# Attention and a two-layer MLP in one kernel: the first batch's up units spread over its bursts, left output halves first, stores by halves, and v ahead of half a weight

## The chip, the cores and the metric

The kernel runs on one core of a Trainium2 chip. A core has a matrix engine (PE, TensorE; PEld is its weight load), a vector engine (DVE), a scalar engine (ACT), a general engine (POOL, GpSimd) and a queue engine (SP, SyncE). Each works through its own list of instructions in order; semaphores hold one engine back for another. DMA transfers are issued from SP, ACT or POOL and run on 16 DMA engines that all queues share. The metric is the device time of one execution in microseconds (us), as the median of several runs.

## What is computed

There are 8 batches, 12 heads, 448 tokens and a head width of 64; q, k and v come as float32 and the output is float32.

```python
q_n, k_n = rmsnorm(q, g_q), rmsnorm(k, g_k)      # over the head width
scores = matmul(q_n, k_n.T) / sqrt(64)
attn = exp(scores - max); attn = attn / (sum(attn) + 1e-9)
x = matmul(attn, v)                              # -> (8*448, 12*64) = (3584, 768)
h = x @ w_in                                     # w_in (768, 2048)
g = maximum(h, 0) + alpha * minimum(h, 0)        # alpha per column of h
out = g @ w_out                                  # w_out (2048, 768)
```

## The kernel before, in words

The twelve heads of a batch are split in two halves g of six, which lie on the lower and the upper 64 partitions. A pair y is two heads (`par`) of each half, four heads in all: y = 0 to 23, three pairs to a batch (G = 3). The 448 tokens are 7 blocks of 64 keys (J = 7). A tile (y, j) is one block of keys of one pair against all queries.

*Preparing a pair.* `load_qk(y)` (L95) loads q and k of a pair on the SP queue into `nat` (six buffers, so three pairs). `square` (L139; ACT for the first two pairs, then POOL), `reduce` (L149, DVE) and `root` (L157, ACT) give the inverse root mean square, `scale` (L166; POOL, some on DVE) multiplies and casts to fp16. Then the block is transposed: for pairs 0 to 5 by PE into PSUM and copied by DVE (`turn`, L186), from pair 6 on by a DMA transpose on SP (`turn_dma`, L176), after which `turn` only multiplies k by the gain on DVE (L190).

*Attention.* `score(y, j)` (L223) makes eight matmuls of 64 rows by 32 columns on parts of the array, into one of two `sc` buffers in PSUM. `soft` (L240, ACT) takes the exponential with a constant bias, no maximum. `den` (L265) sums the exponentials over keys with a matrix of ones, and `attv` (L281) multiplies them with v; both run through `over_keys` (L248) for a couple of pairs (y, y+1) or for the third pair alone, 56 matmuls of 64x32 each; for two pairs, `attv` runs twice. `log` and `invert` (ACT) make the reciprocal of the sum, and DVE multiplies (L306, L308) into `xT`.

*MLP.* `up(b, ft)` (L340) is one of 16 column blocks of the first layer for a batch: six matmuls 128x128x448, an ACT scaling by alpha (L350), a DVE maximum (L351) into `gT`. For batch 0 the first four units are begun early by `begin` (L331). `down(b0, t, oh)` (L355) is one half (oh = 0 left, 1 right) of the 768 output columns for 128 tokens: 16 matmuls 128x128x384, then a DVE copy into `osb` (L371). The output of a token tile is stored after its second half, by two DMAs on SP (L377).

*Banks.* PSUM gives two `sc` tiles (two banks each), one tile `acc` of two banks (den, attv, PE transposes of pairs 3 to 5, and up or down units marked `spare`), and two single banks `mm`.

*Order.* The program is written out in bursts, numbered n, by a planner that runs when the kernel is built. It cuts the 168 tiles into bursts of two, or three in bursts marked `late` (L416), and decides which burst holds a `den` (`den_at`) or `attv` (`av_at`). The lists `prep` and `post` (`at`, `after`, L433, L436) place loads, squares and reduces before or after a burst. From the costs UP = 1.13, DOWN = 2.6 and `cost(n)` (L488) it then deals out up and down units into the `gaps` of the bursts (L499 to L530): a unit is added to a burst until the clock of the costs passes the burst's even share. For batch 0 only the up units count toward that share (`mlp`, L507), and units shorter than UP are never cut short (L528). Of the six down units of batch 0 (three token tiles), four follow in its own period, left half and right half of a tile in turn.

The main loop (L587) then emits, per burst: `prep`; the scores and exponentials; `den` or `attv`; the third tile; roots, scales and DMA transposes; `log` and `invert`; the units of the gap, some of them in the spare bank (L640); `post`. In a burst with plain tiles the second exponential is emitted only after the first up unit (`wait`, L603). Burst 10 is `lead`: there `den` and `attv` of pair 2 come first, then the tiles of pair 3, with the begun up units of batch 0 between.

Weights come over POOL's queue: four parts of `w_in` after bursts 0, 5, 7, 8; the left half of `w_out` (two DMAs of 768 KB) after burst 10 and the right half after burst 11 (L583); v of batch 1 is asked for in burst 12 (L471). POOL issues them in order with its squares and scales.

Of the kernel before, what the change touches and what calls it, by code (L numbers as in the profile page):

```python
# [9 lines left out]
FP32 = mybir.dt.float32  # L10
FP16 = mybir.dt.float16
# [10 lines left out]
def kernel(  # L22
# [12 lines left out]
    nc = tc.nc  # L35
# [35 lines left out]
    nc.vector.memset(expb, EXP_BIAS)  # L71
    epsb = cst.tile([128, 1], FP32, name="epsb", tag="epsb")
    nc.vector.memset(epsb, RMS_EPS)
    ones = cst.tile([128, 32], FP16, name="ones", tag="ones")
    nc.vector.memset(ones, 1.0)
    ident = cst.tile([128, 128], FP16, name="ident", tag="ident")
    make_identity(nc, ident)
# [145 lines left out]
    def score(y, j):  # L223
        qT, kT = qkT[y, "q"], qkT[y, "k"]
        sc = pss.tile([128, 2, 512], FP32, name="sc", tag="sc")
        for c in range(2):
            for par in range(2):
                for g in range(2):
                    nc.tensor.matmul(  # L229
                        out=sc[ds(64 * g + 32 * c, 32), par, :S].rearrange(  # L230
                            "p (j c) -> p j c", j=J
                        ),
                        lhsT=kT[ds(64 * par, 64), j, g, ts(c, 32)],
                        rhs=qT[ds(64 * par, 64), :, g, :],
                        start=True,
                        stop=True,
                    )
        scs[y, j] = sc
# [8 lines left out]

    def over_keys(accs, ys, weights):  # L248

        if len(ys) == 2:  # L250
            heads = [(y, par, 0) for y in ys for par in range(2)]
        else:
            heads = [(ys[0], par, c) for par in range(2) for c in range(2)]
        for j in range(J):
            for h, (y, par, c) in enumerate(heads):
                for g in range(2):
                    nc.tensor.matmul(  # L257
                        out=accs[g][ds(32 * h, 32), :S],
                        lhsT=weights(g, y, par, c, j),
                        rhs=expT[y][ds(64 * g, 64), j, par, :],  # L260
                        start=(j == 0),
                        stop=(j == J - 1),
                    )

    def den(ys):  # L265
        dn = psa.tile([128, 2, 512], FP32, name="dn", tag="acc")
        over_keys(
            (dn[:, 0], dn[:, 1]), ys, lambda g, y, par, c, j: ones[ds(64 * g, 64), :]
        )
        rden[ys] = dn  # L270

# [9 lines left out]
    def attv(ys, half, spare=False, jobs=()):  # L281

        b, i = divmod(ys[0], G)
        v2 = vt[b].rearrange("p h j (d e) -> p h j d e", e=2)

        def weights(g, y, par, c, j):
            h = 2 * (y - G * b) + par
            if len(ys) == 1:
                return vt[b][ds(64 * g, 64), h, j, ts(c, 32)]
            return v2[ds(64 * g, 64), h, j, :, half]  # L290

        if half:
            av, accs = None, [psf.tile([128, 512], FP32, name="avb", tag="mm") for _ in range(2)]
        else:
            pool, tag = (pss, "sc") if spare else (psa, "acc")
            av = pool.tile([128, 2, 512], FP32, name="av", tag=tag)
            accs = (av[:, 0], av[:, 1])
        over_keys(accs, ys, weights)
        for f in jobs:
            f(ys)  # L300
        if b not in xT:
            xT[b] = att.tile([128, 2, G, S], FP16, name="xT", tag="xT")
        x, r = xT[b][:, :, i + half, :], rden[ys]
        if half:
            for g in range(2):
                nc.vector.tensor_mul(out=x[:, g], in0=accs[g][:, :S], in1=r[:, g])  # L306
        else:
            nc.vector.tensor_mul(out=x, in0=av[:, :, :S], in1=r)  # L308
# [41 lines left out]
        nc.scalar.activation(out=ah, in_=hT[:, :S], func=AF.Copy, scale=alpha_sb[:, ft : ft + 1])  # L350
        nc.vector.tensor_max(out=gT[:, ft, ds((b & 1) * S, S)], in0=hT[:, :S], in1=ah)  # L351

    osb = {}

    def down(b0, t, oh, jobs=(), spare=False):  # L355

        op = bank("op", spare)
        for ft in range(NF):
            nc.tensor.matmul(  # L359
                out=op[:, :OH],  # L360
                lhsT=gT[:, ft, ts(t, 128)],
                rhs=w_out_sb[:, ft, ds(oh * OH, OH)],
                start=(ft == 0),
                stop=(ft == NF - 1),
            )
        for f, a in jobs:
            f(*a)
        if oh == 0:
            osb[b0, t] = ffn.tile([128, DM], FP32, name="osb", tag="osb", bufs=2)
        o = osb[b0, t]  # L370
        nc.vector.tensor_copy(out=o[:, ds(oh * OH, OH)], in_=op[:, :OH])  # L371
        last = (b0, t) == (B - 2, J - 1)
        if oh == 1 or last:
            cols_out = ds(oh * OH, OH) if last else slice(None)
            for half in range(2):
                bb, j = divmod(2 * t + half, J)
                (nc.scalar if last and half else nc.sync).dma_start(  # L377
                    out=out4[b0 + bb, j, :, cols_out], in_=o[ds(64 * half, 64), cols_out]
                )

    def spin(count):

# [17 lines left out]
    while m < NG * J or steps:  # L400
        n = len(bursts)
        while steps:
            ys, values = steps[0]
            if values:

                if n in dens and ys != (G - 1,):
                    break
                avs[n] = ys
                av_at.update((y, n) for y in ys)
            else:  # L410
                if n in avs or any(last_in.get(y, n) >= n for y in ys):
                    break
                dens[n] = ys
                den_at.update((y, n) for y in ys)
            steps.pop(0)
        late = len(avs.get(n, ())) == 2 or any(y >= G for y in dens.get(n, avs.get(n, ())))  # L416
        bursts.append([])
        while len(bursts[n]) < (3 if late else 2) and m < NG * J:
            y, j = divmod(m, J)
            if j == 0 and y >= EB and av_at.get(y - EB, n) == n:  # L420

                if y - EB not in av_at:
                    break
                split[n] = min(len(bursts[n]), 2)
            bursts[n].append((y, j))
            first_in.setdefault(y, n)
            if j == J - 1:
                last_in[y] = n
            m += 1
# [17 lines left out]
    for y in range(G, NG):  # L447

        early = y < G + 2
        if early:  # L450
            n = turn_at[y - 1] + (y == G)
        elif y == G + 2:
            n = den_at[G - 1]
        elif y == 2 * G:
            n = turn_at[y] - 4
        elif y == 2 * G + 1:
            n = den_at[G] - 1
        elif y % G:
            n = den_at[y - 3 if y % G == 1 else y - G]
        else:  # L460
            n = av_at[y - 4]
        at(n - (6 if early else 5), load_qk, y)
        for nm in "qk":
            (after if early else at)(n - 2, square, y, nm)
            if early:
                after(n, reduce, y, nm)
            else:
                jobs.setdefault(n, []).append((reduce, (y, nm)))
        roots[n + 1] = y
# [7 lines left out]
    for b in range(B):  # L477
        ups = [(UP / 3 if b == 0 and ft < 4 else UP, up, (b, ft)) for ft in range(NF)]
        odd = b % 2
        new = [  # L480
            (DOWN, down, (b - odd, t, oh))
            for t in (range(3, J) if odd else range(3)) for oh in range(2)
        ]
        tail = len(new) if b == B - 1 else 4 if b == 0 else 2 if odd else 1
        periods.append((ups, carry, new[:tail]))
        carry = new[tail:]
# [12 lines left out]
    for b in range(B - 1):  # L499
# [4 lines left out]
        if b == 0:  # L504

            stop -= len(new)
            mlp = sum(u[0] for u in ups)  # L507
        per = (mlp + sum(cost(n) for n in range(lo, stop))) / (stop - lo)
        clock = 0.0
        for n in range(lo, hi):  # L510
            clock += cost(n)
            free = True
            while ups or old or new:
# [11 lines left out]
                ahead = 0.5 * (UP if ups else DOWN)  # L525
                if not (ups or old) and n + len(new) < hi:
                    break
                short = n in turns and len(gaps[n]) < 2 or u[0] < UP  # L528
                if n < stop - 1 and not short and clock + ahead > per * (n - lo + 1):
                    break  # L530
    ups, old, new = periods[B - 1]
    rest = []
# [47 lines left out]
    after(7, load_w_in, 2)  # L580
    after(8, load_w_in, 3)
    for c in range(4):
        after(first + c // 2, load_w_out, c)  # L583
    roots[3] = 2

    since = 2
    for n in range(NB):  # L587
# [2 lines left out]
        tiles = bursts[n]  # L590

        lead = n == den_at[G - 1]
        if lead:
            den(dens[n])
            attv(avs[n], 0, True, (log, invert))
        first_tiles = tiles[: split.get(n, 2)]
        for t in first_tiles:
            score(*t)
            if lead and t == tiles[0]:
                begin(1)  # L600
                begin(2)
        plain = lead or n not in dens and n not in avs
        wait = plain and not lead and gaps[n] and gaps[n][0][0] is up  # L603
        if lead:
            begin(3)
        for t in tiles[:1] if wait else first_tiles:
            soft(*t)
        if n in dens and not lead:
            den(dens[n])
# [23 lines left out]
        done = 0  # L633

        spare_at, clock = [], 0.0
        taken = n + 1 in dens or n + 1 in avs
        for k, (f, a) in enumerate(gaps[n]):
            free = 2.3 if n in dens else (0.1, 1.2, 0.0)[len(avs.get(n, ()))]
            since += 1
# [73 lines left out]
```

## Time and profile before

| | |
|---|---|
| median of 7 runs | 443.62 us (439.07 to 445.33) |
| the profiled execution | 441.08 us |
| its span, first to last instruction | 439.3 us, mean granted clock of PE 0.996 |
| PE busy | 416.2 us, 5381 matmuls and as many weight loads |
| ACT, DVE, POOL busy | 277.7, 211.9, 176.0 us |
| DMA | 53.89 MB, mean 123 GB/s |
| exponential of one tile (L243) | 1.005 us, 168 of them |
| up unit, down unit on PE (chain of work) | 1.13 us, 2.60 us |

Times in a profile count from the span's first instruction. A row of a timeline gives the start, the length, the engine (PEq, SPq and so on for an engine's queue), the line, the operation, the tile written and the tiles read, and in square brackets the idle time before it and what ended it; "issue" stands for a wait that the profile puts down to nothing else. A busy PE is not a PE at its peak. In part 2 of the page each digit is the busy share of one fortieth of the span in tenths.

### The profile page before, as it was taken

How to read it: one execution, taken by the hardware profiler on the slowest of the kernel's cores; microseconds unless marked ns; L12 is line 12 of the kernel's file. 1: busy time of each engine (PE TensorE's matmuls, PEld its weight loads, DVE VectorE, ACT ScalarE, POOL GpSimd, SP SyncE). 2: the span in 40 equal slices, each digit the busy share in tenths (PEclk: the TensorE clock that was granted, in tenths of full speed). 3: DMA queues.
4: the chain of work that ended last, by engine and by line, in shares of the span. 5: the costliest groups of instructions: out<-in, count | busy, mean ns of one | idle time of the engine just before them, and what ended most of it. 6: DMA issues, size and time to landing. Idle time of an engine off the chain costs nothing.

```text
span 439.3 us, 12178 instructions
## 1 busy us (share of the span) xinstructions
PE 416.2 (95%) x5381; PEld 215.1 (49%) x5381; DVE 211.9 (48%) x303; ACT 277.7 (63%) x385; POOL 176.0 (40%) x133
## 2 busy tenths in 40 slices
PE   7877888999997999999999999999999999999996
PEld 3334334454454545554554545554555545555563
DVE  3655655365664356445545356445544253333421
ACT  4895788578875687767746587767747586222300
POOL 5799793847273631556153632556043000000000
PEclk9899999999999999999999999999999999999999
DMA  8999999988327961678119751775118201111122
GB/s 210 231 207 221 161 248 196 175 170 204 85 60 118 214 161 39 122 183 210 36 28 221 153 154 39 126 181 126 36 27 167 67 2 37 39 36 37 36 73 72
DMA packets 65909, 53.89 MB, mean 123 GB/s; under 512 B 36528, under 2 KB 62400, under 8 KB 65856
## 3 DMA queue, kind: packets, MB, share of 16 engines
q1 hardware_dynamic: 51136, 40.19, 38.3%
q0 software_dynamic: 13984, 11.81, 18.4%
q10 hardware_dynamic: 736, 1.11, 1.0%
q8 instruction: 42, 0.69, 0.7%
q14 instruction: 11, 0.09, 0.1%
HBM read 45.62 MB, written 11.01 MB: 129 GB/s over the span
## 4 chain that ended last, share of the span: by engine, by line
PE 75%; DMA 9%; issue 5%; ACT 4%; DVE 3%; POOL 2%; SPq 2%; POOLq 0%; DVEq 0%; ACTq 0%
PE op L359 25%; PE hT L323 17%; PE hTa L323 9%; PE sc L229 7%; PE opa L359 5%; DMA vt<-in_v_dram 4%; PE dn L257 4%; PE av L257 4%; ACT expT L243 3%; DMA nat<-in_q_dram 2%; PE avb L257 2%; DMA kT<-qs 2%; DMA nat<-in_k_dram 1%; POOL qs L169 1%; SPq L103 1%
## 5 line engine op out<-in xcount | busy, mean ns | idle before, releaser
L243 ACT ACTIVATE expT<-sc,expb 128x896 f16<-128x896 f32 x168 | 160.8, 1005 | 35.8 <-PE sc L229 34.6
L359 PE MATMUL op<-w_out_sb,gT 128*128 128x384 f16 x736 | 127.1, 326 | 0.8 <-issue 0.8
L169 POOL TENSOR_TENSOR qs<-nat,rr 128x896 f16<-128x896 f32 x44 | 76.9, 1766 | 126.3 <-ACT rr L164 96.2
L359 PEld LDWEIGHTS <-gT 128*128 128x128 f16 x896 | 84.6, 98 | 67.6 <-issue 14.0
L323 PEld LDWEIGHTS <-w_in_sb 128*128 128x128 f16 x768 | 73.0, 98 | 75.5 <-issue 11.8
L323 PE MATMUL hT<-xT,w_in_sb 128*128 128x448 f16 x516 | 108.8, 353 | 0.4 <-DVE gT L351 0.4
L350 ACT ACTIVATE ah<-hT,cols 128x448 f16<-128x448 f32 x86 | 54.4, 634 | 55.5 <-PE hT L323 55.5
L146 POOL TENSOR_TENSOR sq<-nat 128x896 f32<-128x896 f32 x44 | 73.5, 1687 | 37.4 <-DMA nat<-in_q_dram 18.5
L351 DVE TENSOR_TENSOR gT<-hT,ah 128x448 f16<-128x448 f32 x86 | 53.6, 624 | 63.3 <-ACT ah L350 63.1
L229 PE MATMUL sc<-qT,kT 64*32 64x448 f16 x1344 | 54.1, 356 | 8.4 <-ACT expT L243 5.6
L371 DVE COPY osb<-op 128x384 f32<-128x384 f32 x46 | 25.6, 556 | 71.2 <-PE op L359 71.2
L323 PE MATMUL hTa<-xT,w_in_sb 128*128 128x448 f16 x240 | 51.9, 352 | 2.5 <-DVE xT L308 2.5
L152 DVE TENSOR_REDUCE ss<-sq 128x14 f32<-128x896 f32 x48 | 50.0, 1076 | 7.0 <-ACT sq L144 6.1
L350 ACT ACTIVATE ah<-hTa,cols 128x448 f16<-128x448 f32 x40 | 25.4, 635 | 30.9 <-PE hTa L323 30.9
L351 DVE TENSOR_TENSOR gT<-hTa,ah 128x448 f16<-128x448 f32 x40 | 25.0, 624 | 25.5 <-ACT ah L350 25.5
L229 PEld LDWEIGHTS <-kT 64*32 64x32 f16 x1344 | 15.7, 89 | 39.1 <-issue 34.1
L359 PE MATMUL opa<-w_out_sb,gT 128*128 128x384 f16 x160 | 27.7, 326 | 0.0
L257 PEld LDWEIGHTS <-vt 64*32 64x32 f16 x1344 | 19.7, 93 | 14.6 <-issue 2.1
L308 DVE TENSOR_TENSOR xT<-av,rden 128x896 f16<-128x896 f32 x16 | 17.4, 1090 | 19.0 <-PE av L257 16.3
L257 PE MATMUL av<-expT,vt 64*32 64x448 f16 x896 | 24.7, 349 | 1.7 <-ACT rden L274 0.9
L257 PE MATMUL dn<-expT,ones 64*32 64x448 f16 x896 | 24.5, 349 | 1.5 <-issue 0.8
L190 DVE TENSOR_SCALAR kT<-kT,gain 128x896 f16<-128x896 f16 x18 | 16.6, 924 | 12.0 <-DMA kT<-qs 12.0
(43 smaller groups left out, 166.0 us busy)
## 6 DMA issues: line engine op xcount, KB each, us to landing
out_dram<-osb SPq DMA_DIRECT2D x54, 192.0 KB, 2.7
nat<-in_q_dram SPq DMA_DIRECT2D x46, 224.0 KB, 4.9
nat<-in_k_dram SPq DMA_DIRECT2D x46, 224.0 KB, 5.4
vt<-in_v_dram POOLq DMA_DIRECT2D x16, 336.0 KB, 6.9
w_in_sb<-in_moe_w_in_dram POOLq DMA_DIRECT2D x12, 256.0 KB, 7.8
w_out_sb<-in_moe_w_out_dram POOLq DMA_DIRECT2D x4, 768.0 KB, 14.5
nat<-in_q_dram ACTq DMA_DIRECT2D x2, 224.0 KB, 4.5
nat<-in_k_dram ACTq DMA_DIRECT2D x2, 224.0 KB, 5.5
```

What stands on the lines that cost most here:

```text
L146: nc.gpsimd.tensor_mul(out=sqf, in0=src, in1=src)
L152: nc.vector.tensor_reduce(out=ss_t[y][:, "qk".index(nm)].rearrange("p h j -> p (h j)").unsqueeze(2), in_=sqs[y, nm], axis=AXIS_X, op=ALU.add,)
L169: eng.tensor_mul(out=t.rearrange("p j h d -> p h j d"), in0=nat[y, nm], in1=rr_t[y][:, "qk".index(nm)].unsqueeze(3).broadcast_to((128, 2, ...
L229: nc.tensor.matmul(out=sc[ds(64 * g + 32 * c, 32), par, :S].rearrange("p (j c) -> p j c", j=J), lhsT=kT[ds(64 * par, 64), j, g, ts(c, 32)] ...
L243: nc.scalar.activation(out=expT[y][:, j], in_=scs[y, j][:, :, :S], func=AF.Exp, scale=QK_SCALE, bias=expb[:, 0:1],)
L257: nc.tensor.matmul(out=accs[g][ds(32 * h, 32), :S], lhsT=weights(g, y, par, c, j), rhs=expT[y][ds(64 * g, 64), j, par, :], start=(j == 0), ...
L308: nc.vector.tensor_mul(out=x, in0=av[:, :, :S], in1=r)
L323: nc.tensor.matmul(out=hT[:, :S], lhsT=w_in_sb[:, g * G + i, ts(ft, 128)], rhs=xT[b][:, g, i, :], start=(i == 0 and g == 0), stop=(i == G ...
L350: nc.scalar.activation(out=ah, in_=hT[:, :S], func=AF.Copy, scale=alpha_sb[:, ft : ft + 1])
L351: nc.vector.tensor_max(out=gT[:, ft, ds((b & 1) * S, S)], in0=hT[:, :S], in1=ah)
L359: nc.tensor.matmul(out=op[:, :OH], lhsT=gT[:, ft, ts(t, 128)], rhs=w_out_sb[:, ft, ds(oh * OH, OH)], start=(ft == 0), stop=(ft == NF - 1),)
L371: nc.vector.tensor_copy(out=o[:, ds(oh * OH, OH)], in_=op[:, :OH])
```

## The change

- `score` takes 64 keys in one piece instead of two of 32 for the pairs of batch 0 (y < 3): four matmuls of 64x64 instead of eight of 64x32. `den` and `attv` of pair 2 do the same. `ones` is widened to 64 columns.
- In burst 10 (`lead`) the first tile's score and exponential stand ahead of `den` and `attv`, the begun units follow the second tile, and the burst takes three tiles instead of two. There are then 72 bursts instead of 73.
- The up units of batch 0 are dealt out by a count that rises evenly over its bursts (`goal`), and the down units come after them. Of the down units of batch 0, the three left halves come first. For the other batches the rule that ends a burst's units is changed a little.
- A `down` unit has an `osb` tile of its own for half the columns (four buffers) and stores it at once, by two DMAs of half the width.
- The loads of q and k for pairs 5 to 9 are placed up to one burst later; the right half of `w_out` is asked for after burst 12 instead of 11, and so behind v of batch 1.
- The spare bank is not taken by a burst's last unit if the next burst has a transpose on PE.

```diff
     def score(y, j):
...
-        for c in range(2):
+        m = 64 if y < G else 32
+        for c in range(64 // m):
...
-                        out=sc[ds(64 * g + 32 * c, 32), par, :S].rearrange(
+                        out=sc[ds(64 * g + m * c, m), par, :S].rearrange(
...
-                        lhsT=kT[ds(64 * par, 64), j, g, ts(c, 32)],
+                        lhsT=kT[ds(64 * par, 64), j, g, ts(c, m)],
...
     def over_keys(accs, ys, weights):
+        m = 64 if ys == (G - 1,) else 32
...
-            heads = [(ys[0], par, c) for par in range(2) for c in range(2)]
+            heads = [(ys[0], par, c) for par in range(2) for c in range(64 // m)]
...
-                        out=accs[g][ds(32 * h, 32), :S],
-                        lhsT=weights(g, y, par, c, j),
+                        out=accs[g][ds(m * h, m), :S],
+                        lhsT=weights(g, y, par, ts(c, m), j),
...
-        if oh == 0:
-            osb[b0, t] = ffn.tile([128, DM], FP32, name="osb", tag="osb", bufs=2)
-        o = osb[b0, t]
-        nc.vector.tensor_copy(out=o[:, ds(oh * OH, OH)], in_=op[:, :OH])
+        o = ffn.tile([128, OH], FP32, name="osb", tag="osb", bufs=4)
+        nc.vector.tensor_copy(out=o, in_=op[:, :OH])
         last = (b0, t) == (B - 2, J - 1)
-        if oh == 1 or last:
-            cols_out = ds(oh * OH, OH) if last else slice(None)
-            for half in range(2):
-                bb, j = divmod(2 * t + half, J)
-                (nc.scalar if last and half else nc.sync).dma_start(
-                    out=out4[b0 + bb, j, :, cols_out], in_=o[ds(64 * half, 64), cols_out]
-                )
+        for half in range(2):
+            bb, j = divmod(2 * t + half, J)
+            (nc.scalar if last and half else nc.sync).dma_start(
+                out=out4[b0 + bb, j, :, ds(oh * OH, OH)], in_=o[ds(64 * half, 64)]
+            )
...
-        late = len(avs.get(n, ())) == 2 or any(y >= G for y in dens.get(n, avs.get(n, ())))
+        late = len(avs.get(n, ())) == 2 or n in dens and n in avs or any(y >= G for y in dens.get(n, avs.get(n, ())))
...
-        at(n - (6 if early else 5), load_qk, y)
+        at(n - (6 if early else 4 if y <= 3 * G else 5), load_qk, y)
...
+        if b == 0:
+            new.sort(key=lambda u: u[2][2])
...
-            mlp = sum(u[0] for u in ups)
...
-                short = n in turns and len(gaps[n]) < 2 or u[0] < UP
-                if n < stop - 1 and not short and clock + ahead > per * (n - lo + 1):
+                if b == 0:
+                    goal = 5 + round((NF - 5) * (n - lo) / (stop - 1 - lo))
+                    if NF - len(ups) >= goal and n < stop - 1:
+                        break
+                    continue
+                short = n in turns and len(gaps[n]) < 2
+                if n < hi - 1 and not short and clock + ahead > per * (n - lo + 1):
                     break
...
-        after(first + c // 2, load_w_out, c)
+        after(first + c // 2 * 2, load_w_out, c)
...
-        if lead:
-            den(dens[n])
-            attv(avs[n], 0, True, (log, invert))
-        first_tiles = tiles[: split.get(n, 2)]
+        first_tiles = tiles[: split.get(n, 2)] if not lead else tiles
         for t in first_tiles:
             score(*t)
             if lead and t == tiles[0]:
+                soft(*t)
+                den(dens[n])
+                attv(avs[n], 0, True, (log, invert))
+            elif lead and t == tiles[1]:
                 begin(1)
                 begin(2)
...
-        for t in tiles[:1] if wait else first_tiles:
+        for t in tiles[:1] if wait else tiles[1:] if lead else first_tiles:
             soft(*t)
...
-        taken = n + 1 in dens or n + 1 in avs
+        taken = n + 1 in dens or n + 1 in avs or turns.get(n + 1, TD) < TD
```

More of the change, by code (lines that the diff above doesn't have):

```diff
@@ L73 @@
     nc.vector.memset(epsb, RMS_EPS)
-    ones = cst.tile([128, 32], FP16, name="ones", tag="ones")
+    ones = cst.tile([128, 64], FP16, name="ones", tag="ones")
     nc.vector.memset(ones, 1.0)
@@ L267, in den @@
         over_keys(
-            (dn[:, 0], dn[:, 1]), ys, lambda g, y, par, c, j: ones[ds(64 * g, 64), :]
+            (dn[:, 0], dn[:, 1]), ys, lambda g, y, par, c, j: ones[ds(64 * g, 64), c]
         )
@@ L288, in weights @@
             if len(ys) == 1:
-                return vt[b][ds(64 * g, 64), h, j, ts(c, 32)]
+                return vt[b][ds(64 * g, 64), h, j, c]
             return v2[ds(64 * g, 64), h, j, :, half]
@@ L351, in up @@
         nc.vector.tensor_max(out=gT[:, ft, ds((b & 1) * S, S)], in0=hT[:, :S], in1=ah)
-    osb = {}
     def down(b0, t, oh, jobs=(), spare=False):
```

## The prediction

> **What bounds the kernel now.** I read the page's first two parts, then busy time by stage, then what TensorE (PE) waited for, then the timelines around each wait.
>
> ```profile
> PE 416.2 (95%) x5381; PEld 215.1 (49%) x5381; DVE 211.9 (48%) x303; ACT 277.7 (63%) x385; POOL 176.0 (40%) x133
> ...
> PE   7877888999997999999999999999999999999996
> ```
>
> PE is the bound, but not from the start: its slices are full only from the eighth (77 us) on, but for one. By stage (PE, PEld, DVE, ACT, POOL busy, then clock, DMA share, GB/s):
>
> ```profile
> 27.20:38.60 11.40, 8.19 (x243) 4.60 (x242) 5.93 (x8) 9.47 (x12) 11.36 (x11) 1.00 1.15 250
> 38.60:46.70 8.10, 6.88 (x145) 3.38 (x146) 5.35 (x6) 4.16 (x7) 5.19 (x5) 1.00 1.11 175
> 46.70:72.20 25.50, 20.75 (x209) 9.74 (x208) 13.14 (x22) 19.86 (x32) 21.49 (x16) 1.00 1.14 210
> 72.20:82.30 10.10, 8.88 (x234) 4.61 (x234) 4.39 (x6) 8.68 (x12) 3.29 (x2) 1.00 1.23 168
> 82.30:138.00 55.70, 55.55 (x837) 28.64 (x837) 29.88 (x41) 42.62 (x58) 29.65 (x22) 1.00 0.70 138
> 138.00:142.00 4.00, 1.54 (x10) 0.74 (x9) 4.00 (x4) 0.00 (x0) 3.27 (x2) 1.00 0.17 37
> ```
>
> From 82 us PE idles only once for over a microsecond. So a gain can come from three places: 27 to 47, 47 to 82, and 138 to 142. PE's waits there, from its timeline (start, length, what; idle time before it and its releaser):
>
> ```profile
> 34.73 0.37 PE L229 MATMUL sc<-qT,kT 64*32 64x448 f16 x5 [1.38 <-issue]
> ...
> 40.92 0.76 PE L257 MATMUL dn<-expT,ones 64*32 64x448 f16 x23 [0.81 <-issue]
> ...
> 53.01 0.38 PE L229 MATMUL sc<-qT,kT 64*32 64x448 f16 x8 [1.50 <-ACT expT L243]
> ...
> 60.29 0.38 PE L229 MATMUL sc<-qT,kT 64*32 64x448 f16 x8 [1.31 <-ACT expT L243]
> ...
> 69.02 0.94 PE L204 MATMUL tps<-ident,qs 128*128 128x128 f16 x14 [0.80 <-DVE gT L351]
> ...
> 78.85 1.52 PE L257 MATMUL av<-expT,vt 64*32 64x448 f16 x55 [0.86 <-DMA vt<-in_v_dram]
> ...
> 141.24 1.29 PE L323 MATMUL hTa<-xT,w_in_sb 128*128 128x448 f16 x6 [2.46 <-DVE xT L308]
> ```
>
> All PE waits after 13 us sum to 15.1 us; that is the purse. I followed the planner's lists through the old and new code to see which burst holds what.
>
> **64 keys in one piece (first three pairs).** The two "issue" waits fall after 700 and 956 PE instructions, 256 apart. The instruction queue carries 42 packets and 0.69 MB, 16 KB each, and PE has 2 x 5381 instructions: 256 a packet. So PE waited for its own program. The packets began at 31.97 and 38.56, and PE went on 2.8 and 2.4 us later, while DMA was full (share 1.15). The Trainium skill ("Runtime: NRT & Kernel Launch", Instruction fetch mechanics) calls crossing such a block mostly hidden. By that rule fewer instructions save nothing; by the rows up to 1.38 + 0.81. I follow the rows. The change drops 4 matmul and load pairs in each of 21 tiles and 28 in each of one den and one attv: 140 pairs, 280 instructions. The 700th then falls into turn(3) at about 35.7 us, the 956th into burst 11, where a block lasts over 6 us. For the first I leave 0.4 us of stall. Gain 2.19 - 0.4 = 1.8; ends 0 (the stalls only move) and 2.7 (the 0.55 before dn goes too).
>
> What 64 columns cost PE no row shows. Nearest row: 64x32 pieces, 56 in 1.32 us, 8 in 0.19 us, which is eight sub-arrays at once. Four 64-wide pieces cover the same array: 0.19 again, and I take that. Bad end: halves in turn, 0.38, so 21 x 0.19 = 4.0 us (under the 0.92 us spacing of the exponentials, nearly hidden) plus 2 x 1.32 = 2.6 us at burst 10, exposed. A gain is excluded: 448 columns pass either way. Two rules speak against it. "TensorE: Matmul & The Clock Gate", LDWEIGHTS, prices a load by its columns, P / 1.2 ns: four loads of 64 would be 213 ns a tile, 24 more than 189, over 21 + 14 groups 0.8 us. But it gives the same 213 for eight loads of 32, where the trace has 189; the row stands: 0. "TensorEngine Tiling", Key Properties, says a mode switch drains the array. The trace agrees: a first up unit after scores takes 1.24, not 1.13, so 0.11. New switches between 64- and 32-wide: six in bursts 7 to 9, where PE idles anyway, two in burst 10: 0.22. One burst fewer (73 to 72) takes away two: 0.22. Net 0.
>
> **Burst 10 reordered.** score and exp (3,0) now stand ahead of den, and three tiles run instead of two. ACT idled 3.17 us there waiting for dn; the moved exponential (1.0 us) lies in that hole. Nothing is priced for it: its gain shows below, as ACT being less late. PE's cost is one tile moved, not added. Cover gone, it would delay den by 0.4.
>
> **Ups spread evenly.** Up units in bursts 11 to 16 were 1, 2, 1, 3, 2, 2; now 2, 2, 3, 2, 2 and a down unit. Rows: tile pair 0.51 on PE, 0.92 each on ACT; up 1.13 on PE (+0.11), 0.52 on ACT; turn 0.79 on PE; root 0.49 on ACT. A burst with one up is 1.75 on PE and 2.36 (2.85 with a root) on ACT: PE must wait. With two it is 2.89 against 2.88: even. The 1.50 and 1.31 us waits stand right behind the two bursts with one up. The 0.80 stands where a turn wants the bank that a spare up unit holds; the changed `taken` keeps spare off before turns. Together 3.61 of 4.82 us of PE waits in this stage. ACT's sum in bursts 11 to 16 (12 x 0.92 + 11 x 0.52 + 2 x 0.49 = 17.7) stays under PE's (20.9), so it can be filled. I take 3.0; ends 1.0 and 4.8.
>
> **v before the right half, left halves first.** v of batch 1 was issued at 60.31 behind 3 MB of w_out (issued 50.1 to 57.0) and took 16.3 and 17.8 us. Now 1.5 MB lie ahead, and POOL reaches v at about 56. At the 190 GB/s that this stretch moved it lands near 68; attv wants it near 76. The 0.86 goes, and the 0.20 "issue" behind it. But a block boundary now falls into avb at about 77, with a fetch asked for at 70.5; at the 6 to 8 us that fetches took in full DMA, half a microsecond stalls. Gain 0.5; ends -0.5 and 1.1. The right half is moved past v on POOL's queue, issued near 57.6, and lands near 76; it is wanted by the fourth down unit near 84, as the three left halves come first. If it were late, every us is on PE. w_out's left half (landed 9.7 and 14.3 us after its issue) is wanted near 67, issued near 48: 4 us of room.
>
> **Later batches.** The same units, cut a tile earlier and grouped anew, in a stage where PE is 98% busy (292.44 of 297.30): 0, end -1.0, one new wait of the kind at 60.
>
> **Loads of q, k a burst later.** SP works in order, and its loads wait for buffers, not for their place: old load 5 went out at 25.09 when its buffer came free. Order among them is kept: 0. **Stores by halves:** 56 more issues of about 0.54 us on SP, 30 us over 350, on a queue idle most of the time. A store waits for its copy; behind it stand the next loads and transposes, which belong to later bursts. Load 10 waited for a store until 94.69; now it stands behind an earlier one. 0, end -0.5 (cover gone, 1.1 us for each transpose behind a pair). `ones` at 64 columns: a 0.09 us memset at 0.9 us, hidden.
>
> **The wait at 141.** DVE held a kT at 137.79 after waiting 6.22 us for its transpose, because v of batch 3 was issued at 130.10, beside that transpose (130.19, landing 7.58 later; 2.7 is usual):
>
> ```profile
> 137.79 1.93 DVE L190 TENSOR_SCALAR kT<-kT,gain 128x896 f16<-128x896 f16 x1 [6.22 <-DMA kT<-qs]
> ...
> 130.10 1.35 POOL L112 DMA_DIRECT2D vt<-in_v_dram  x2
> ```
>
> New lists put square(12), 3.3 us of POOL, between scale(10) and load_v(3), and scale(10) a burst earlier. The transpose is through before v starts. For v of batches 4 and 6 the pattern appears, but with two down units behind, as v of batch 5 had before (kT took 6.6 us, no wait for it on PE). Gain 2.4; ends 0 and 2.5.
>
> **Sum.** 1.8 + 3.0 + 0.5 + 2.4 = 7.7 us. The profiled execution took 441.08 us, 439.3 of it span; it would take 433.4. The median, 443.62, lies 2.5 above it; minus 7.7 it gives 435.9, say 436.0.
>
> **Rivals.**
> - *DMA sets the pace.* w_out, v and two q, k loads (5.7 MB) saturate DMA until 79, whatever their order. Pair 6's k transpose, last of them, landed at 81.18, and its first score stood at 84.9. If it still lands there, bursts 17 to 19 gain at most 84.9 - 81.6 = 3.3; with the later gain failing too, 440.3. For it: DMA share over 1.1 from 27 to 82. Against: DMA moved 175 GB/s from 38.6 to 46.7, and w_out is now asked for some 2 us earlier. Chance 0.17.
> - *Slower: the transposes of pair 6 behind the right half.* Old q landed at 78.85, when v's last bytes did (78.81): transposes crawl beside big loads. Now the right half is what they crawl beside, and POOL's scale(7) waits for q as well (it idled 9.18 for it). Score(6,0) is due near 81; each later us is PE's. With the other gains kept, it decides when k lands after some 89 us; at 94 the time is 449. Against: no byte is added. Chance 0.08.
> - *64-wide pieces don't overlap:* 2.6 exposed and some of the 4.0: 439. Chance 0.07.
> - *As forecast:* 0.68.
>
> A measurement of this kernel tells about 1% (4.4 us) from no change. The forecast's cases lie below 439.2 but for a tail of 0.02, half of the third rival too: faster 0.70. Of the slower rival 0.01 stays under 1%: slower 0.07, same 0.23. Low end: all PE waits named above gone, 12 us: 431.5. High end: reaches past the first rival, 442.5.
>
> **What would show it.** PE's idle after 13 us falls from 15 to some 7 to 8 us; no 1.4 us "issue" wait at 33; no waits over 1 us on exponentials between 50 and 70; attv of pairs 3, 4 not released by v; nothing at the place of 141. Wrong if score(6,0) is released by a late kT, if 64x64 pieces are 0.38 us a group of four, or if "issue" waits reappear.

## The result, and the profile after

The changed kernel took 438.97 us in the median of 24 runs, the kernel before 442.7 us in 61. The ratio, taken from the fast runs of both and so not exactly that of the two medians, is 0.9911, with a 95% interval of 0.9889 to 0.9933. It is 0.9% faster, 3.9 us (3.0 to 4.9). The forecast was 436.0, a gain of 7.7 us. The time lies in the range, the direction is right, and half of the forecast gain is missing. The profiled executions give the same picture: 437.14 us with a span of 435.4, against 441.08 with 439.3, which is 3.9 us of span.

First the changed kernel's page, busy time by engine and PE in fortieths of the span:

```profile
PE 417.1 (96%) x5241; PEld 215.4 (49%) x5241; DVE 209.1 (48%) x303; ACT 277.5 (64%) x385; POOL 175.7 (40%) x133
...
PE   8779999799999999999999999999999999999996
```

PE is full from the fourth slice on instead of the eighth, and the dip near 140 is gone. But there is a new dip in the eighth slice, at 76 to 87 us. Busy time by stage (columns as before: stretch, its length, PE, PEld, DVE, ACT, POOL, clock, DMA share, GB/s):

```profile
27.20:36.70 9.50, 8.00 (x215) 4.09 (x214) 5.53 (x8) 8.98 (x12) 9.48 (x8) 1.00 1.16 239
36.70:43.50 6.80, 6.25 (x94) 2.99 (x93) 4.92 (x7) 4.67 (x6) 6.78 (x8) 1.00 1.15 207
43.50:69.22 25.72, 24.01 (x221) 11.53 (x219) 16.61 (x25) 21.51 (x35) 22.70 (x18) 1.00 1.18 216
69.22:80.87 11.65, 11.17 (x249) 6.00 (x249) 3.82 (x7) 7.68 (x10) 5.59 (x4) 1.00 1.28 173
80.87:90.49 9.62, 6.91 (x99) 3.08 (x98) 3.00 (x4) 4.67 (x5) 4.68 (x4) 0.82 1.17 194
90.49:138.00 47.51, 47.51 (x735) 24.16 (x734) 27.53 (x38) 37.98 (x54) 23.64 (x16) 1.00 0.67 143
```

The stage up to the end of batch 0's up units had 4.75 us of idle PE in 25.50; now it has 1.71 in 25.72, and a down unit is done inside it. The fifth row is the surprise: 2.71 us of idle PE in 9.62, and a mean granted clock of 0.82. PE's timeline there, the two small waits of the stage before it, and the places of the old waits in den of pair 2, on v and at 141:

```profile
37.71 1.52 PE L259 MATMUL dn<-expT,ones 64*64 64x448 f16 x28
...
50.61 0.38 PE L230 MATMUL sc<-qT,kT 64*32 64x448 f16 x8 [0.51 <-ACT expT L244]
...
66.20 0.38 PE L230 MATMUL sc<-qT,kT 64*32 64x448 f16 x8 [0.45 <-ACT expT L244]
...
74.33 1.51 PE L259 MATMUL av<-expT,vt 64*32 64x448 f16 x56
...
76.92 1.32 PE L259 MATMUL avb<-expT,vt 64*32 64x448 f16 x44 [0.48 <-issue]
...
81.59 1.50 PE L259 MATMUL dn<-expT,ones 64*32 64x448 f16 x52
85.66 0.44 PE L259 MATMUL dn<-expT,ones 64*32 64x448 f16 x4 [2.56 <-issue]
85.67 0.80 PE L230 MATMUL sc<-qT,kT 64*32 64x448 f16 x8
86.40 4.15 PE L359 MATMUL op<-w_out_sb,gT 128*128 128x384 f16 x16
...
136.53 1.30 PE L325 MATMUL hTa<-xT,w_in_sb 128*128 128x448 f16 x6
```

In den of pair 5 PE stops for 2.56 us, four matmuls before its end, waiting for nothing that the profile shows. Then a down unit takes 4.15 us instead of 2.77. The clock says why:

```profile
80.90:85.60 4.70, 2.05 (x69) 0.97 (x68) 2.54 (x3) 1.91 (x2) 3.79 (x3) 1.00 1.21 180
85.60:89.20 3.60, 3.54 (x21) 1.48 (x22) 0.45 (x1) 2.63 (x3) 0.90 (x2) 0.53 1.11 205
```

After the stop PE was granted half its clock for 3.4 us. The stop and the slow down unit together cost 2.56 + (4.15 - 2.77) = 3.9 us, which is the missing gain; the scores between them, at half clock, cost some 0.4 us more.

The ledger, by where equal work stands in the two profiles (equal but for one or two score tiles, of 0.19 us each):

| stage | before | after | gain |
|---|---|---|---|
| first up unit of burst 11 | 49.71 | 47.30 | 2.4 |
| from it to den of pairs 3, 4 (after: with a down unit of 2.7 more) | 23.2 | 22.3 | 3.6 |
| from that to the next burst with plain scores, two down units in it | 12.0 | 11.3 | 0.7 |
| from there to the first up unit of batch 1 (what is left of the difference) | | | -4.4 |
| from there to the first up unit of batch 2 | 43.2 | 40.8 | 2.4 |
| from there to the end | 298.1 | 298.8 | -0.8 |

That is 3.9 us. PE's waits after 13 us, those over 0.15 us, fell from 15.1 to 10.7 us, not to 7 or 8. At 81 us the kernel was 6.7 us ahead, more than forecast; ten microseconds later it was 2.3 us ahead.

### The profile page after: what moved, and what is told of

Read it like the earlier page. It is cut to its first block, busy times and chain, and to the rows that moved or that the text cites. A ratio compares the mean times of both kernels' runs of the same rounds, so it can differ in the third digit from the quotient of the medians.

```text
span 435.4 us, 12032 instructions
## 1 busy us (share of the span) xinstructions
PE 417.1 (96%) x5241; PEld 215.4 (49%) x5241; DVE 209.1 (48%) x303; ACT 277.5 (64%) x385; POOL 175.7 (40%) x133
## 4 chain that ended last, share of the span: by engine, by line
PE 87%; ACT 6%; DVE 3%; issue 1%; DMA 1%; SPq 0%; ACTq 0%
PE op L359 29%; PE hT L325 20%; PE hTa L325 10%; PE sc L230 8%; PE opa L359 6%; PE dn L259 5%; PE av L259 5%; ACT expT L244 3%; PE avb L259 3%; DMA nat<-in_k_dram 1%; ACT ah L352 1%; DVE ss L152 1%; DVE gT L353 1%; PE tps L204 1%; DVE kT L215 0%
## 5 line engine op out<-in xcount | busy, mean ns | idle before, releaser
L359 PE MATMUL op<-w_out_sb,gT 128*128 128x384 f16 x752 | 130.9, 329 | 0.0
L230 PE MATMUL sc<-qT,kT 64*32 64x448 f16 (+1 forms) x1260 | 53.7, 356 | 6.3 <-ACT expT L244 4.3
L230 PEld LDWEIGHTS <-kT 64*32 64x32 f16 (+1 forms) x1260 | 15.3, 90 | 37.1 <-issue 31.7
L259 PE MATMUL dn<-expT,ones 64*32 64x448 f16 (+1 forms) x868 | 24.6, 350 | 3.4 <-issue 2.6
L259 PEld LDWEIGHTS <-vt 64*32 64x32 f16 (+1 forms) x1316 | 19.6, 93 | 14.0 <-issue 2.7
L259 PE MATMUL av<-expT,vt 64*32 64x448 f16 (+1 forms) x868 | 24.3, 349 | 0.7 <-ACT rden L276 0.7
L359 PE MATMUL opa<-w_out_sb,gT 128*128 128x384 f16 x144 | 24.9, 326 | 0.0
L259 PEld LDWEIGHTS <-ones 64*32 64x32 f16 (+1 forms) x868 | 13.0, 93 | 12.2 <-issue 4.8
## 6 DMA issues: line engine op xcount, KB each, us to landing
w_out_sb<-in_moe_w_out_dram POOLq DMA_DIRECT2D x4, 768.0 KB, 15.1
```

Of the source, the lines that this page charges most:

```text
L230: nc.tensor.matmul(out=sc[ds(64 * g + m * c, m), par, :S].rearrange("p (j c) -> p j c", j=J), lhsT=kT[ds(64 * par, 64), j, g, ts(c, m)], r ...
L259: nc.tensor.matmul(out=accs[g][ds(m * h, m), :S], lhsT=weights(g, y, par, ts(c, m), j), rhs=expT[y][ds(64 * g, 64), j, par, :], start=(j = ...
L359: nc.tensor.matmul(out=op[:, :OH], lhsT=gT[:, ft, ts(t, 128)], rhs=w_out_sb[:, ft, ds(oh * OH, OH)], start=(ft == 0), stop=(ft == NF - 1),)
```

## The experiments

My theory after this (F): PE's program comes in blocks of 256 instructions over DMA; in a full DMA stretch a block comes late, and PE stops when its end falls into a dense run of small matmuls. The stop stands after 1978 PE instructions, counted in the trace; the stops of the kernel before stood after 700 and 956, which is 5 x 256 and 4 x 256 fewer, but for 2 instructions. The rival (D): this stretch of time is congested by transposes, stores or weights, and PE would stop there whatever its program.

**Fewer instructions at the place of the stop.**

```diff
 def over_keys(accs, ys, weights):
-    m = 64 if ys == (G - 1,) else 32
+    m = 64 if ys in ((G - 1,), (2 * G - 1,)) else 32
```

> The changed kernel with 64-wide pieces also in den and attv of pair 5 (28 matmuls each in place of 56). Theory F (PE runs out of program: a block of 256 instructions is fetched when the one before it is entered, and comes late while DMA is full): den of pair 5 then holds 56 instructions instead of 112, the block's end falls to the end of the down unit behind it, near 86 us, and the fetch is there by then. The 2.56 us wait in dn at 82.7 goes or shrinks below 0.7, the granted clock stays at 1.0 behind it, and the time falls by 3 to 4 us against the changed kernel, to about 435. Rival D (the wait belongs to the stretch of time, whatever the instruction count: transposes of pair 7, right half of w_out, stores): PE still stops for 2 to 3 us between 80 and 87, and the time stays at 439.

It took 433.67 us, a ratio of 0.9823 (0.9765 to 0.9881) to the kernel before. PE in this run:

```profile
81.41 1.52 PE L259 MATMUL dn<-expT,ones 64*64 64x448 f16 x28
82.86 0.38 PE L230 MATMUL sc<-qT,kT 64*32 64x448 f16 x8
83.18 2.77 PE L359 MATMUL op<-w_out_sb,gT 128*128 128x384 f16 x16
```

No stop and no cold clock there: the pieces cover the same columns in half the instructions. The comparison that counts is with the changed kernel on one chip, so both were run again together.

> The kernel with 64-wide pieces in den and attv of pair 5, once more beside the changed kernel on one chip: 3.5 to 5.5 us under the changed kernel if the wait in dn and the cold clock behind it are what separates them, 433 to 435. If the earlier run was a lucky one, within 2 us of it.

> The changed kernel once more, for the comparison on one chip: ratio to the kernel before 0.989 to 0.993, a wait of 2 to 4 us on 'issue' in dn of pair 5, with or without a cold clock behind it.

434.24 us (ratio 0.9809, 0.9766 to 0.9851) against 438.15 (0.9923, 0.9887 to 0.9959): 3.9 us apart. The slowest of its six runs, 435.55, is faster than the fastest of the twelve of the changed kernel, 436.32. The changed kernel showed the stop again, at the same matmul, and the cold clock:

```profile
82.21 1.50 PE L259 MATMUL dn<-expT,ones 64*32 64x448 f16 x52
85.85 0.37 PE L259 MATMUL dn<-expT,ones 64*32 64x448 f16 x4 [2.14 <-issue]
85.87 0.55 PE L230 MATMUL sc<-qT,kT 64*32 64x448 f16 x8
86.34 4.46 PE L359 MATMUL op<-w_out_sb,gT 128*128 128x384 f16 x16
```

The version with the wide pieces in pair 5 beats both kernels. In its second profile the block's end still cost something, at the score tiles behind the down unit:

```profile
87.89 0.57 PE L230 MATMUL sc<-qT,kT 64*32 64x448 f16 x16 [0.72 <-ACT rden L281]
```

The operation named there had ended 0.56 us earlier; the place is again after 1978 instructions, and the packet of the next block had begun at 85.37 us, 2.5 us before.

**More instructions early, the same PE work.**

```diff
-            spin(4)
+            spin(16, 4)     # four times as many, a quarter of the columns each
```

> The changed kernel with each warming matmul of bursts 0 to 6 cut into four of a quarter of the columns: the same PE time, 60 more matmuls and loads, 120 more instructions before 27 us. Theory F: every block end stands 120 instructions earlier in the program, so the wait leaves dn and is found between the avb of pairs 3, 4 and the scores of pair 6, near 79 to 81, as 'issue', of 0.5 to 2.5 us; the earlier small wait leaves avb too. Rival D: the wait stays in dn behind 81.6, at its 2.56 us.

It took 438.64 us (0.9926, 0.9892 to 0.996). PE at the place:

```profile
81.64 0.38 PE L230 MATMUL sc<-qT,kT 64*32 64x448 f16 x8
84.62 0.38 PE L230 MATMUL sc<-qT,kT 64*32 64x448 f16 x8 [2.60 <-issue]
84.82 1.51 PE L259 MATMUL dn<-expT,ones 64*32 64x448 f16 x56
```

The stop left den and stands between the two score tiles ahead of it, 120 instructions earlier in the program and again after 1978 of the run. So it is bound to the count, not to the operation. The trace shows the fetch itself: the 16 KB packet of the next block began at 81.89 us here, and PE went on 2.7 us later, at 84.62. In the two profiles of the changed kernel the packets began at 83.10 and 83.18, and PE went on 2.6 and 2.7 us later. F holds. A second stop of 1.07 us came into the first avb (34.84), where an earlier block now ends. This time no cold clock followed.

**What holds the block back: the new stores?**

```diff
-        for half in range(2):
+        for half in range(0 if b0 == 0 and t < 3 and oh == 0 else 2):
```

> The changed kernel without the six stores of the three left halves of batch 0 (this part of the output is left out). They are 0.6 MB issued from 74 us on, beside the fetch. If the stores by halves delay the fetch, the wait in dn at 82.7 shrinks to under 1 us and the time falls by 2.5 to 4 us, to about 436. If the transposes of pairs 6 and 7 and the right half of w_out delay it, the wait stays above 2 us and the time falls by less than 1 us.

439.29 us (0.9952, 0.9917 to 0.9986), and the stop was longer, 3.93 us:

```profile
86.96 0.56 PE L259 MATMUL dn<-expT,ones 64*32 64x448 f16 x4 [3.93 <-issue]
```

The stores are not it. Without them ahead on SP, q of pair 7 was transposed from 75.98 instead of 78.27, and landed no earlier.

**Or the right half of w_out?**

```diff
-    for c in range(4):
+    for c in range(2):
         after(first + c // 2 * 2, load_w_out, c)
...
-                rhs=w_out_sb[:, ft, ds(oh * OH, OH)],
+                rhs=w_out_sb[:, ft, ds(0, OH)],
```

> The changed kernel without the load of the right half of w_out (1.6 MB issued at 57.5 to 59.3 us left out; the right half of the output is computed with the left half's weights, the same work on PE). If that load is what the fetch and the transposes of pairs 6 and 7 wait behind, the transposes of pair 6 land within 5 us of their issue instead of 11, the wait in dn at 82.7 goes with the cold clock behind it, and the time falls by 3.5 to 4.5 us, to about 434.5. If the transposes alone hold the fetch back, the wait stays above 1.5 us.

432.71 us (0.9804, 0.9774 to 0.9834). The changed kernel did not run on this chip; by the ratios this is 4.7 us under it. The DMA view of 66 to 70 us, issues with their time to landing, first of the changed kernel, then of this one:

```profile
qT<-qs SPq DMA_TRANSPOSE x1, 11.6
kT<-qs SPq DMA_TRANSPOSE x1, 10.9
```

```profile
qT<-qs SPq DMA_TRANSPOSE x1, 3.4
kT<-qs SPq DMA_TRANSPOSE x1, 2.9
```

The stop in den is gone, and from 67 to 202 us PE has no wait over 0.2 us. So the 1.6 MB of the right half, in flight beside the transposes of pair 6, is where the lateness comes from. But it did not stand in the fetch's own way to the end: its last bytes landed at 78.2 us, and the packet began at 83.10. In flight then were transfers held up earlier. The loads of q and k of pair 9 stand behind those transposes on SP, issued from 71.8 us in the changed kernel and from 70.1 here:

```profile
nat<-in_q_dram SPq DMA_DIRECT2D x2, 224.0 KB, 8.7
nat<-in_k_dram SPq DMA_DIRECT2D x2, 224.0 KB, 9.4
```

```profile
nat<-in_q_dram SPq DMA_DIRECT2D x2, 224.0 KB, 4.8
nat<-in_k_dram SPq DMA_DIRECT2D x2, 224.0 KB, 5.4
```

In the changed kernel they landed at 80.3 to 83.3 us; here they landed at 74.1 to 77.5, and the packet of the same block began at 78.16. Which of the held-up transfers (these loads, the stores behind them, the transposes of pair 7) keeps the packet back is not separated. The part that was to relieve v thereby loaded the stretch behind it.

**Even spreading alone undone.**

```diff
-                    goal = 5 + round((NF - 5) * (n - lo) / (stop - 1 - lo))
-                    if NF - len(ups) >= goal and n < stop - 1:
+                    goal = (5, 6, 8, 9, 12, 14, 16)[min(n - lo, 6)]
+                    if ups and NF - len(ups) >= goal:
```

> The changed kernel with the old counts of up units in bursts 11 to 16 (1, 2, 1, 3, 2, 2 instead of 2, 2, 3, 2, 2, 0), the first left half still in burst 16. Theory S (even spreading is what took the waits on exponentials away): waits of about 1.5 us in burst 12 and 1.3 us in burst 14 come back, den of pairs 3, 4 stands 2.0 to 3.0 us later than in the changed kernel. Rival D (DMA sets the pace to 80 us): den stands later, but pair 6's scores don't, since the transposes land at the same time, and the time stays within 1 us of the changed kernel.

```profile
51.16 0.38 PE L230 MATMUL sc<-qT,kT 64*32 64x448 f16 x8 [1.50 <-ACT expT L244]
...
58.43 0.38 PE L230 MATMUL sc<-qT,kT 64*32 64x448 f16 x8 [1.31 <-ACT expT L244]
...
81.12 1.32 PE L259 MATMUL avb<-expT,vt 64*32 64x448 f16 x44 [1.96 <-issue]
...
85.36 0.57 PE L230 MATMUL sc<-qT,kT 64*32 64x448 f16 x16 [0.21 <-DVE kT L190]
...
88.15 0.37 PE L259 MATMUL dn<-expT,ones 64*32 64x448 f16 x4 [0.82 <-issue]
```

Both old waits are back at their old lengths, behind the bursts with one up unit, and den of pairs 3, 4 starts at 72.34 instead of 69.61. (Of these 2.7 us, 0.55 stand there before burst 11, 0.43 of them a late block in turn(3).) Theory S holds for the place. But the time is 439.33 (0.9944, 0.9918 to 0.997), 0.3% from the changed kernel, with intervals that overlap: most of the 2.7 us come back at the next fetches, which stop PE for 2.8 us here and for 3.0 us plus the cold clock in the changed kernel. What spreading gains is in good part spent waiting for the same DMA.

**The order of v and w_out undone.**

```diff
-        after(first + c // 2 * 2, load_w_out, c)
+        after(first + c // 2, load_w_out, c)
```

> The changed kernel with the right half of w_out asked for after burst 11 again, ahead of v of batch 1. Theory of the forecast (v behind 3 MB of w_out lands when attv of pairs 3, 4 already waits): v lands near 77 instead of 67.7 and attv waits for it 1.5 to 3 us, as its place is 3 us earlier than in the kernel before. The wait in dn of pair 5 shrinks by about as much, since the fetch behind it has that time more. Sum: within 1.5 us of the changed kernel. Rival (v's place is worth its whole wait): 2 us or more slower than the changed kernel.

```profile
78.23 0.36 PE L259 MATMUL av<-expT,vt 64*32 64x448 f16 x1 [3.31 <-DMA vt<-in_v_dram]
80.58 2.81 PE L259 MATMUL av<-expT,vt 64*32 64x448 f16 x55 [1.99 <-DMA vt<-in_v_dram]
```

The wait for v was 5.3 us, not 1.5 to 3, and the clock went cold at 80 us; the stop in den of pair 5 vanished, as expected. Time 440.53 (0.9939, 0.9907 to 0.9971): 2.4 us above the changed kernel on that chip, as the rival had it, though the intervals overlap. With everything in front of it earlier, v's place matters more than it did in the kernel before.

**64-wide pieces undone.**

```diff
-    m = 64 if ys == (G - 1,) else 32
+    m = 32
...
-        m = 64 if y < G else 32
+        m = 32
```

> The changed kernel with 32-wide pieces everywhere, as before: 280 more PE instructions up to burst 10. Theory F: an 'issue' wait of 1.0 to 1.8 us comes back at the score behind attv of pairs 0, 1 (33 us) and one of 0.5 to 1 us in den of pair 2; the first up units stand 1.5 to 2.5 us later than in the changed kernel; the late wait stays in dn of pair 5, as 280 is 256 and 24, only 24 instructions earlier. Time 440.5 to 441.5. Rival (64-wide pieces bring nothing): first up units at the same place, time 439.

```profile
35.36 0.37 PE L230 MATMUL sc<-qT,kT 64*32 64x448 f16 x5 [1.64 <-issue]
35.37 2.25 PE L259 MATMUL avb<-expT,vt 64*32 64x448 f16 x56
...
90.63 0.69 PE L259 MATMUL dn<-expT,ones 64*32 64x448 f16 x16 [4.20 <-issue]
```

The stop at the score behind the first attv is back, 1.64 us, with a cold clock behind it (avb 2.25 instead of 1.52). The stop in den of pair 2 did not come: a miss. The late stop stands 12 matmuls earlier in den, with 16 left instead of 4: 24 instructions, as worked out. The first up unit of burst 11 stands 3.2 us later, counted from the first exponential, more than expected because of the clock. Yet the median, 439.13 (0.9941, 0.9902 to 0.9981), cannot be told from the changed kernel's. That the 280 instructions move the stops is shown; that they are worth their 1.8 us in time is not.

**64-wide pieces in every lone den and attv.**

```diff
-    m = 64 if ys == (G - 1,) else 32
+    m = 64 if len(ys) == 1 else 32
```

> The changed kernel with 64-wide pieces in den and attv of the third pair of every batch: 16 times 56 pieces become 28, 392 pairs fewer than in the changed kernel. Theory F: as with pair 5 alone, about 433.5 to 435; later batches gain nothing, since fetches there come in time, so not under 432.5. Rival (64-wide pieces themselves are cheaper on PE): 0.2 us per den and attv, 3 us more, under 431.

436.37 us (0.9879, 0.9851 to 0.9908): slower than with pair 5 alone (0.9823 and 0.9809 on its chips), where I had expected no difference. In its profile pair 6's scores waited 1.51 us for k. And from the first up unit of batch 1 (93.69) to the end it took 341.7 us; with pair 5 alone (91.36) 339.2. That stretch has 12 more 64-wide groups, so 2.5 / 12 = 0.21 us each, two mode switches. Once fetches come in time, wide pieces only cost.

**v of batch 3 away from the transpose, in the kernel before.**

```diff
-        at(av_at[G * b] - 6, load_v, b)
+        at(av_at[G * b] - (5 if b == 3 else 6), load_v, b)
```

> The kernel before, with v of batch 3 asked for one burst later, behind scale(11) on POOL. Theory V (the 2.46 us wait at 141 comes from the k transpose of pair 10 running beside v of batch 3): that transpose lands 2.6 to 2.8 us after its issue instead of 7.6, DVE doesn't wait for it, PE's wait at 141 goes and the time falls by 2.0 to 2.5 us, to about 440.4. Rival: the transpose is slow for its place in the SP queue, the wait stays and so does the time.

```profile
138.88 2.77 PE L359 MATMUL op<-w_out_sb,gT 128*128 128x384 f16 x16
141.49 1.30 PE L323 MATMUL hTa<-xT,w_in_sb 128*128 128x448 f16 x6
```

The wait is gone, and from the first up unit of batch 1 to the end the profile is 2.6 us shorter than before (338.7 against 341.3). The transpose landed 4.15 us after its issue, better than 7.58 but not the 2.7 that I had named. The time doesn't show it: 440.34 (0.9993, 0.995 to 1.0036). In the profiled execution the wait for v of batch 1, far ahead of the edit, was 3.6 us instead of 0.9, with a cold clock behind it, and ate the gain. The mechanism is shown; its worth in the median is not resolved.

## Why the prediction was right, and half too large

*Fewer instructions, burst 10 (forecast 1.8).* In the profile 2.4 us, to the first up unit of burst 11. The 1.38 and 0.81 stops went, and even the 0.4 that I had left did not come in this profile. In the second profile of the changed kernel it came, and was 0.90, after 700 instructions and in turn(3), as forecast:

```profile
36.53 0.56 PE L204 MATMUL tps<-ident,qs 128*128 128x128 f16 x7 [0.90 <-POOL sq L146]
```

The profile names POOL, but the packet of the block had begun at 33.69 us, 2.8 before. The first up unit of burst 11 stands at 48.31 there, a gain of 1.4. That 64-wide pieces cost what 32-wide ones do was right: den of pair 2 took 1.35 us from start to start. So was the price of 0.11 for a switch: the run with all lone groups wide gives 0.21 for two. (The rows show it elsewhere than I read it: not the first but the last up unit before scores takes 1.23 from start to start, and a tile pair before an up unit takes 0.51 instead of 0.39.)

*Spreading (forecast 3.0).* 3.6 us in its stage, by the mechanism named: the 1.50, 1.31 and 0.80 are gone; the first two come back when the counts are undone, the third doesn't, as the rule on spare banks stayed.

*v and the right half (forecast 0.5, from -0.5 to 1.1).* Up to 80 us right: v landed at 67.7, the right half at 78.2, the stop in avb was 0.48, and the stage gained 0.7. Here lies the step that failed: the sum priced one block end behind the moved load, in avb, and stopped there. The next end lies 256 instructions on, in den of pair 5. With the transfers in flight that the right half had held up, the packet did not begin before 83.10, and PE reached the end of its program some 6 us after the stop in avb. That cost 2.56 us of stop and, with the half clock behind it, the 4.4 us of the ledger's fourth row. So the term was not 0.5 but near 0.7 - 4.4 = -3.7. The text named the sign of it ("if 'issue' waits reappear") but gave no price, and its low end of -0.5 was too narrow. The new order is not what costs: with it undone, v alone cost 5.3 us, and the time was 2.4 us longer. What was left out is the price of the second block end.

*The wait at 141 (forecast 2.4).* 2.4 us, for the reason given: square(12) lies between scale(10) and v.

*Later batches (0, end -1.0).* -0.8 in the profile: den of pair 23 waits 0.65 for the bank of a down unit set `spare` right ahead of it, and two up units wait 0.25 each; an old stop of 0.77 at 237.9 is gone. That makes -0.4; the rest has no place that I can name.

*The total.* The first two terms came out 1.2 us above their forecast. Without that, less than half of the forecast gain would have been left; this much was luck.

*The rivals.* The first, that DMA sets the pace to 80 us, had the right cause and the wrong victim: the transposes came in time (79.1, scores of pair 6 at 80.9), PE's program did not. The second named the right half as what transposes crawl beside, which the run without it confirms, but the price fell on the fetch. The third is refuted.

## What to carry to other kernels

In a stretch where DMA is full, the program itself is a transfer with a due time: count the instructions of the densest engine from one stop to the next, and price every block end that falls into a run of small operations, not only the first. A load moved out of one wait's way is in flight beside whatever comes after it. Fewer, wider instructions at just such a place were worth 3.9 us; where the blocks came in time, they cost 0.21 us a group.

## What was not expected of the hardware

Short stops were enough to halve PE's granted clock for the next 3.4 us: 2.14 and 2.56 us in the changed kernel, 1.64 us in the run with 32-wide pieces. But the length of the stop alone does not decide it: after 1.96 us in the run with the old counts, 2.60 us in the run with quartered spins, and 2.46 us at 141 in the kernel before, the clock stayed at full. A late block of 256 instructions cost PE up to 4.20 us. And two DMA transposes that landed in 3.4 and 2.9 us without the right half of w_out took 11.6 and 10.9 with its 1.6 MB in flight.
